# An instruction order made anew: a planner's durations and gaps as a trace shows them, and the 1e-9 of a softmax on ScalarE or VectorE

## The chip, the cores and the metric

The kernel runs on one core of a Trainium2 chip. The metric is the device time of one execution in microseconds (us). The kernel before takes 829.24 us, the median of three runs that lie between 827.79 and 829.8. The execution whose profile is read here took 828.89 us.

The engines are called as in the profile: PE is TensorE (PEld its weight loads), ACT is ScalarE, DVE is VectorE, POOL is GpSimd, and SP is SyncE, which here only starts DMAs.

## The reference

Windowed attention is followed by a gated two-layer product, all in float32:

```python
# q, k, v: (8 batches, 8 heads, 576, 64); mask: 32 keys back, for heads 4..7 every 4th key of 128
scores = where(mask, (q @ k.T) / 8, -1e9)
attn = exp(scores - scores.max(-1))
attn = attn / (attn.sum(-1) + 1e-9)
x = (attn @ v) laid out as (4608 tokens, 512)
h = x @ w_in                          # (4608, 2048)
g = h * (1 / (1 + exp(-1.702 * h)))
out = g @ w_out                       # (4608, 512)
```

## The kernel before, in words

**The products.** A float32 product is made of three products in a faster format (fp32r): each operand is split into a high part and the rest, and high x high, rest x high and high x rest are added. So a step of 128 rows on a tile of 512 tokens is three matmuls of 128x512. Over the whole kernel 3168 such matmuls carry the two layers. The weights arrive as 64-bit words, 16 tiles of w_in (`wi0` to `wi15`) and 16 of w_out, and are decoded on the chip (`decode`): seven passes over each tile by ACT, DVE and POOL, the last two of them writing `wi_kept` or `wo_kept`.

**The stages.** The tokens of a batch are one group of 512 (the last 64 of all the batches make a ninth group). Three groups, m0, m1 and m2, are done plainly: for each of 16 tiles f of the hidden layer, `up` makes `hp_m`(f) with 12 matmuls, ACT and DVE gate it, ACT and DVE or POOL split it (`gh`, `gl`), and 12 matmuls add it to four accumulators `acc_m`. The other six groups are done in three blocks p, q and r of two groups each, by a scheme with seven products of sums of halves in place of eight; its matmuls are `up_p` (or q, r) and `second_p`. In a unit of a block seven products of six matmuls take turns in two PSUM banks, and ACT or DVE empties a bank before it is begun anew. Other matmuls (`acc_m`, `second`) stand between them where there are some.

**The attention.** 32 pairs of heads (four of a batch) are done by small matmuls: `scores` writes `sp`, DVE takes the maximum and subtracts it, ACT takes the exponential (`exponentials`), DVE sums it, adds 1e-9 and takes the reciprocal (`inverse`), DVE or POOL multiplies, DVE transposes in squares of 32, and `product` (for the first batch `first_product`, which writes `first_x`) multiplies by v. `drain_x` copies the result: for the first batch ACT writes the high part into `xs` and DVE the rest. The first batch's four pairs come ahead of everything else, because m0 is made from them; while they run the weights are decoded. In those first microseconds PE also gets matmuls whose results nobody uses (`idle`).

**What sets the order.** Every piece of work is given to `Plan.add` with the engines that could do it and a duration for each, a number of urgency, and what it reads and writes. `Plan.placed` then goes through time with a model of five engines, lays each piece on one of its engines, and writes down the order; `Plan.latest` works out when a piece must start so as not to hold up PE, and the placing is done again three times with these due times. The program is written out in this order, and on the chip every engine works through its own list, in order, waiting on semaphores. So the planner's durations don't set a time on the chip. They choose which engine does a piece, and what stands ahead of what.

Its rules, as far as the change touches them: an engine is free again when its piece ends; the result can be used on another engine after `LATENCY` of that engine, and on the same one 0.13 later (0 on PE). A negative duration of DVE marks a piece that can't run at the same time as one of POOL (`port`). PE's instruction list comes in blocks, which `fetched` models. `idle` matmuls are put in wherever, in the model, PE waits for over half a microsecond in the first 60 us.

Of the kernel before, what the change touches and what calls it, by code (L numbers as in the profile page):

```python
# [10 lines left out]
AF = mybir.ActivationFunctionType  # L11
# [30 lines left out]

PE, ACT, DVE, POOL, DMA = range(5)
LATER = {PE: 0.0, ACT: 0.0, DVE: 0.51, POOL: 0.04, DMA: 0.0}
LATENCY = {PE: 0.3, ACT: 0.2, DVE: 0.2, POOL: 0.2, DMA: 0.2}


class Plan:
# [62 lines left out]
    def placed(self, warm_until, soon, late=None):  # L111
# [22 lines left out]
        def fetched(count, when, cost):  # L134

            n = issued[0]
            issued[0] += count
            for j in range(len(blocks) - 1, 1 << 30):
                edge = 193 + 256 * j
                if edge >= n + count or edge > 1500:  # L140
                    return when + cost
                part = cost * (edge - n) / count
                at = max(when + part, blocks[j])
                blocks.append(at + (6.1 if at < 18.0 else 4.2))
                when, cost, n, count = at, cost - part, edge, count - (edge - n)
# [7 lines left out]
        while any(open_):  # L153
# [41 lines left out]
            starts[i] = when  # L195
            if e == PE:
                cost = fetched(ops[i][5], when, cost) - when
            if e == POOL or (e == DVE and ops[i][0][e] < 0):
                port[0] = when + cost

            free[e] = when + (cost if e != DMA else 0.7 if cost < 100 else 0.43)
            if e == DMA:
                bus[0] = max(bus[0], when + 2.0) + cost / 360.0
                cost = bus[0] - when
            for j in users[i]:
                for to in ready[j]:
                    gap = 0.0 if to == e == PE else 0.13 if to == e else LATENCY[to]
                    ready[j][to] = max(ready[j][to], when + cost + gap + ops[j][4])
                wait[j] -= 1
                if not wait[j]:  # L210
                    for to in ops[j][0]:
                        open_[to].add(j)
# [4 lines left out]
def tile_windowed_attention_then_gated_mlp(  # L217
# [130 lines left out]
    def pair(e, dst, a, b, op):  # L348
        (V if e == DVE else G).tensor_tensor(out=dst, in0=a, in1=b, op=op)  # L349
# [5 lines left out]
    def decode(n, urgency):  # L355
# [30 lines left out]
        def take_sign(e):  # L386
# [7 lines left out]
        add({ACT: 0.66}, urgency, lambda e: A.activation(value, f32(at["top"]), AF.Copy, scale=2.0 ** -112), (R,), (E,))  # L394
        add({ACT: 0.66}, urgency, lambda e: A.activation(
            at["low"], at["low"], AF.Copy, scale=2.0 ** -29), (R,), (R + "l",))
        add({DVE: -0.75, ACT: 1.37}, urgency, take_sign, (R,), (R + "l",))
        add({DVE: -0.43}, urgency, lambda e: V.tensor_scalar(
            out=word, in0=word, scalar1=3, scalar2=None, op0=ALU.logical_shift_left), (), (E,))
        add({DVE: -0.70, POOL: 1.33}, urgency, lambda e: pair(e, word, word, at["low"], ALU.add), (R + "l",), (E,))  # L400
# [106 lines left out]

    def inverse(k, urgency):
        sm, SM = sms[turn(k)], f"sm{turn(k)}"
        add({DVE: -0.15}, urgency, lambda e: V.tensor_scalar(  # L510
            out=sm, in0=sm, scalar1=1.0e-9, scalar2=None, op0=ALU.add), (), (SM,))
        add({DVE: 0.19}, urgency, lambda e: V.reciprocal(out=sm, in_=sm), (), (SM,))  # L512

    def softmax(k, urgency):

        y = turn(k)
        pr, sm, ct = prs[y], sms[y], cts[y]
        PR, SM, CT = (f"{n}{y}" for n in ("pr", "sm", "ct"))
        exponentials(k, urgency)
        add({DVE: 0.80}, urgency, lambda e: V.tensor_reduce(out=sm, in_=pr, axis=AX.X, op=ALU.add), (PR,), (SM,))  # L520
        inverse(k, urgency)
        for a in range(2):
            add({POOL: 0.85, DVE: -0.48}, urgency, lambda e, a=a: pair(
                e, pr[:, a], pr[:, a], sm[:, a, :, None].broadcast_to([P, QT, W]), ALU.mult), (SM,), (f"{PR}.{a}",))
        if k < NC:

            for a in range(2):
                to = ct.rearrange("p h t a q -> p (h t a q)")[:, a * QT * W:a * QT * W + QT * W]
                add({DVE: 0.48}, urgency, lambda e, a=a, to=to: V.transpose(
                    out=to, in_=pr[:, a].rearrange("p t w -> p (t w)")), (PR, f"{PR}.{a}"), (f"{CT}.{a}",))  # L530
            return
        for half in (0, 1):
            add({DVE: 0.42}, urgency, lambda e, half=half: V.transpose(  # L533
                out=ct[:, half].rearrange("p t a q -> p a t q"), in_=pr[:, :, :, 32 - 32 * half:64 - 32 * half]),
                (PR, f"{PR}.0", f"{PR}.1"), (f"{CT}.{half}",))

        for m in range(8):
            j, prev = m % 4, m // 4  # L540
            odd, upper = j % 2, j // 2
            row = D * upper + 32 * (odd != prev)
            col = 32 * odd if not prev or odd else 64
            shift = prev and not odd
            tiles = slice(1 if shift and not upper else 0, QT - upper)
            to = slice(1, QT) if upper and not shift else slice(0, tiles.stop - tiles.start)
            dst = bt[row:row + 32, to, :, col:col + 32]
            src = ct[32 * j:32 * j + 32, prev, tiles]

            def work(e, dst=dst, src=src):  # L550
                if e == DMA:
                    load(dst, src)
                else:
                    copy(e, dst, src)

            costs = {DMA: 82} if k < FIRST * NC else {ACT: 0.49, DVE: -0.33}
            add(costs, urgency, work, (f"{CT}.{prev}",), (f"bt.{m}",))

    def first_product(k):
# [732 lines left out]
```

## Time and profile before

| what | us |
|---|---|
| median of three runs | 829.24 (827.79 to 829.8) |
| the profiled execution | 828.89 |
| its span, first to last instruction | 827.2 |
| PE busy | 811.2 (98%) |
| DVE busy | 669.7 (81%) |
| ACT busy | 515.0 (62%) |
| POOL busy | 327.8 (40%) |
| mean busy share of the DMA queue q1 | 69.3% |

The span is 1.7 us shorter than the execution's time. A share of busy time is a mean over stages: PE is idle for 7.9 us of the first 40 and for 4.8 us of the last 27, and hardly anywhere else. Matmuls overlap, and their ends are modelled, so a wait of PE begins earlier than the idle time that a row shows.

### The profile page before, as it was taken

To read this page: it belongs to the slowest core of one execution; us is meant where nothing else is said; L and a number is where in the kernel's file an instruction comes from. 1 tells how busy PE (TensorE), PEld (TensorE's weight loads), DVE (VectorE), ACT (ScalarE), POOL (GpSimd) and SP (SyncE) were. 2 spreads that over 40 slices of the span, in tenths; PEclk is the share of its full clock that TensorE was granted. 3 is DMA by queue.
4 is the path that set the end of the run, shared out by engine and by line. 5 is a ranking of instruction groups with operands and counts; after the bars stand their busy time and mean duration, and the time that the engine had idled before them with its cause. 6 is when DMAs were issued, how large, how long until landed. Compare 5 with 4: busy or idle time off the path is not lost.

```text
span 827.2 us, 18837 instructions
## 1 busy us (share of the span) xinstructions
PE 811.2 (98%) x7240; PEld 653.5 (79%) x7240; DVE 669.7 (81%) x1104; ACT 515.0 (62%) x992; POOL 327.8 (40%) x296
## 2 busy tenths in 40 slices
PE   7899999999999999999999999999999999999997
PEld 4678777888878888878788788888888888888886
DVE  6898989787888778898989998977679876867575
ACT  7998986676676777586776655446446544544340
POOL 3343336566655663324235357331125431112251
PEclk8799999999999999999999999999999999999999
DMA  9476658889757567868878878675665658664546
GB/s 359 152 244 193 181 192 287 295 281 314 249 189 254 183 200 257 267 190 280 279 229 261 261 233 260 219 269 168 214 193 182 211 186 273 203 222 149 189 151 181
DMA packets 109610, 188.12 MB, mean 227 GB/s; under 512 B 26448, under 2 KB 55376, under 8 KB 109520
## 3 DMA queue, kind: packets, MB, share of 16 engines
q1 hardware_dynamic: 109376, 186.78, 69.3%
q8 instruction: 57, 0.93, 0.5%
q14 instruction: 33, 0.27, 0.1%
q10 hardware_dynamic: 144, 0.13, 0.0%
HBM read 140.64 MB, written 45.09 MB: 225 GB/s over the span
## 4 chain that ended last, share of the span: by engine, by line
PE 88%; DVE 7%; ACT 1%; issue 1%; DMA 1%; SPq 0%; DVEq 0%; ACTq 0%
PE hp_m L848 15%; PE up_q L991 9%; PE up_r L991 9%; PE up_p L991 8%; PE second_q_Q L1106 5%; PE second_r_Q L1106 5%; PE second_p_Q L1106 5%; PE acc_m L785 5%; PE acc_m L789 5%; PE acc_m L786 4%; PE sp L482 3%; PE second_r_Z L1106 3%; PE second_R L1106 3%; PE second_q_Z L1106 3%; PE second_p_Z L1106 2%; PE av L607 2%
## 5 line engine op out<-in xcount | busy, mean ns | idle before, releaser
L349 POOL TENSOR_TENSOR arena<-arena 128x256 f32<-128x256 f32 (+3 forms) x109 | 118.0, 1091 | 155.7 <-DVE wi_last_units L349 34.7
L848 PE MATMUL hp_m<-xs,wi_kept 128*128 128x512 f32 x504 | 129.1, 398 | 0.7 <-DVE xs L349 0.4
L848 PEld LDWEIGHTS hp_m<-xs,wi_kept 128*128 128x128 f32 x504 | 93.3, 188 | 22.5 <-DVE arena L857 1.6
L342 ACT ACTIVATE wo_kept<-arena 128x512 fp32r<-128x512 f32 x115 | 71.9, 629 | 42.3 <-PE second_r_Q L1106 11.4
L349 POOL TENSOR_TENSOR wo_kept<-arena,wo_kept 128x512 fp32r<-128x512 f32 x34 | 45.3, 1340 | 105.5 <-ACT wo_kept L342 72.2
L991 PE MATMUL up_p<-wi_kept,xs 128*128 128x512 f32 x336 | 84.7, 394 | 2.2 <-DVE arena L349 1.3
L991 PE MATMUL up_r<-wi_kept,xs 128*128 128x512 f32 x336 | 85.3, 389 | 0.0
L991 PE MATMUL up_q<-wi_kept,xs 128*128 128x512 f32 x336 | 83.4, 389 | 0.0
L991 PEld LDWEIGHTS up_p<-wi_kept,xs 128*128 128x128 f32 x336 | 62.1, 188 | 16.8 <-DVE arena L349 2.2
L991 PEld LDWEIGHTS up_q<-wi_kept,xs 128*128 128x128 f32 x336 | 63.0, 188 | 13.4 <-DVE arena L1013 0.3
L991 PEld LDWEIGHTS up_r<-wi_kept,xs 128*128 128x128 f32 x336 | 63.1, 188 | 13.1
L349 DVE TENSOR_TENSOR wo_kept<-arena,wo_kept 128x512 fp32r<-128x512 f32 x87 | 65.3, 761 | 5.9 <-ACT wo_kept L342 5.4
L349 POOL TENSOR_TENSOR wo_kept<-wi_last_units,wo_kept 128x512 fp32r<-128x512 f32 x23 | 31.9, 1388 | 84.6 <-ACT wo_kept L342 84.6
L785 PE MATMUL acc_m<-gh,wo_kept 128*128 128x512 f32 x156 | 61.7, 395 | 0.4 <-ACT arena L342 0.3
L786 PE MATMUL acc_m<-gh,wo_kept 128*128 128x512 f32 x156 | 60.9, 390 | 0.0
L349 POOL TENSOR_TENSOR pr<-pr,sm 128x320 f32<-128x320 f32 x52 | 43.3, 850 | 43.0 <-DVE sm L512 29.3
L342 ACT ACTIVATE bt<-ct 32x256 f32<-32x256 f32 (+1 forms) x127 | 55.2, 435 | 3.2 <-DVE ct L533 0.9
L1012 ACT ACTIVATE arena<-arena 128x512 f32<-128x512 f32 x60 | 37.5, 628 | 28.9 <-DVE arena L349 25.1
L349 DVE TENSOR_TENSOR gl<-arena,gh 128x512 fp32r<-128x512 f32 x53 | 44.9, 847 | 9.1 <-PE acc_m L789 6.4
L349 DVE TENSOR_TENSOR arena<-arena 128x512 f32<-128x512 f32 (+1 forms) x68 | 50.4, 747 | 0.4
L1013 DVE SCALAR_TENSOR_TENSOR arena<-arena 128x512 f32<-128x512 f32 x60 | 48.1, 807 | 0.7 <-ACT arena L1012 0.2
L342 ACT ACTIVATE wo_kept<-wi_last_units 128x512 fp32r<-128x512 f32 x47 | 29.6, 629 | 30.0 <-PE second_r_Z L1106 8.9
(261 smaller groups left out, 1826.6 us busy)
## 6 DMA issues: line engine op xcount, KB each, us to landing
xs<-sums SPq DMA_DIRECT2D x168, 256.0 KB, 3.3
out_weights<-sums_o SPq DMA_DIRECT2D x63, 512.0 KB, 3.8
qk<-qk_dram SPq DMA_DIRECT2D x29, 576.0 KB, 5.2
xs<-sums_o SPq DMA_DIRECT2D x21, 512.0 KB, 3.6
v<-vp_dram SPq DMA_DIRECT2D x28, 320.0 KB, 4.4
sums<-arena SPq DMA_DIRECT2D x32, 256.0 KB, 3.6
sums_o<-arena SPq DMA_DIRECT2D x32, 256.0 KB, 3.4
arena<-wi_dram SPq DMA_DIRECT2D x15, 512.0 KB, 4.7
```

Source lines behind the costliest of these rows:

```text
L342: A.activation(dst, src, AF.Copy, scale=scale)
L349: (V if e == DVE else G).tensor_tensor(out=dst, in0=a, in1=b, op=op)
L482: T.matmul(dst[:, w:w + n], u["qk"][rows, at:at + 32], u["qk"][rows, S + first:S + first + n], start=not masked(k), stop=True, tile_positi ...
L607: T.matmul(u["x"][i][rows, at:at + last - first], u["v"][keys, a, m], bt[keys, m, a, first:last], start=(bank_, a) not in begun, stop=True ...
L785: T.matmul(self.acc[j], w[:, 0, cols], high, start=f == 0, stop=False)
L786: T.matmul(self.acc[j], w[:, 1, cols], high, start=False, stop=False)
L789: T.matmul(self.acc[j], w[:, 0, P * j:P * j + P], low, start=False, stop=f == NF - 1)
L848: T.matmul(hps[f], wi(f)[:, st, cols], mv[:, c], start=c == 0 and k == 0, stop=c == NC - 1 and k == 2)
L991: T.matmul(self.banks[place], xs[:, slot, at:at + P], wi_kept[:, 2 * a + c, mv], start=fresh and c == 0 and k == 0, stop=c == 1 and k == 2 ...
L1012: add({ACT: 0.60}, -10.0, lambda e: A.activation(unit(tmp), src(), AF.Tanh, scale=0.851), need, own(tmp))
L1013: add({DVE: -0.70 if need[0][0] == "A" else 0.70}, -10.0, lambda e: V.scalar_tensor_tensor(out=unit(dst), in0=unit(tmp), scalar=1.0, in1=s ...
L1106: T.matmul(self.second[key], w[:, st, cols], mv, start=fresh and y == 0 and k == 0, stop=y == 1 and k == 2, skip_group_check=True)
```

## The change

The planner's numbers are changed, and with them the order of all five engines' lists. Results are handed on sooner in the model (`LATENCY`, with exceptions in `FROM`), and ACT, DVE and POOL are free for their next piece a little before a piece ends (`LEAVES`). The durations of some pieces are set anew. And the addition of 1e-9 to the sums of a softmax, which DVE alone could do, may be done by ACT too, as a copy with a bias.

```diff
 LATER = {PE: 0.0, ACT: 0.0, DVE: 0.51, POOL: 0.04, DMA: 0.0}
-LATENCY = {PE: 0.3, ACT: 0.2, DVE: 0.2, POOL: 0.2, DMA: 0.2}
+LATENCY = {PE: 0.06, ACT: 0.04, DVE: 0.04, POOL: 0.09, DMA: 0.2}
+FROM = {PE: {ACT: 0.2, DVE: 0.2}, DMA: {PE: 0.3, ACT: 0.2, DVE: 0.2, POOL: 0.2}}
+LEAVES = {PE: 0.0, ACT: 0.10, DVE: 0.085, POOL: 0.045, DMA: 0.0}
...
+            leaves = when + cost - min(LEAVES[e], 0.6 * cost)
             if e == POOL or (e == DVE and ops[i][0][e] < 0):
-                port[0] = when + cost
-
-            free[e] = when + (cost if e != DMA else 0.7 if cost < 100 else 0.43)
+                port[0] = leaves
+
+            free[e] = leaves if e != DMA else when + (0.7 if cost < 100 else 0.43)
...
-                    gap = 0.0 if to == e == PE else 0.13 if to == e else LATENCY[to]
+                    gap = 0.0 if to == e == PE else FROM.get(e, {}).get(to, LATENCY[to])
...
-        add({DVE: -0.75, ACT: 1.37}, urgency, take_sign, (R,), (R + "l",))
+        add({DVE: -0.65, ACT: 1.22}, urgency, take_sign, (R,), (R + "l",))
...
-        add({DVE: -0.15}, urgency, lambda e: V.tensor_scalar(
-            out=sm, in0=sm, scalar1=1.0e-9, scalar2=None, op0=ALU.add), (), (SM,))
+        def shift(e):
+            if e == ACT:
+                A.activation(sm, sm, AF.Copy, bias=1.0e-9)
+            else:
+                V.tensor_scalar(out=sm, in0=sm, scalar1=1.0e-9, scalar2=None, op0=ALU.add)
+
+        add({ACT: 0.2, DVE: -0.15}, urgency, shift, (), (SM,))
...
-            add({POOL: 0.85, DVE: -0.48}, urgency, lambda e, a=a: pair(
+            add({POOL: 0.73, DVE: -0.48}, urgency, lambda e, a=a: pair(
...
-                add({DVE: 0.48}, urgency, lambda e, a=a, to=to: V.transpose(
+                add({DVE: 0.50}, urgency, lambda e, a=a, to=to: V.transpose(
...
-            add({DVE: 0.42}, urgency, lambda e, half=half: V.transpose(
+            add({DVE: 0.50}, urgency, lambda e, half=half: V.transpose(
...
-            costs = {DMA: 82} if k < FIRST * NC else {ACT: 0.49, DVE: -0.33}
+            costs = {DMA: 82} if k < FIRST * NC else {ACT: 0.45, DVE: -0.29}
```

Over the whole program the amount of work is the same but for `idle` matmuls of 128x512, of which there are 30 before and 12 now. Work moves between engines: 31 of the 32 additions of 1e-9 go from DVE to ACT; of the additions, subtractions and products of two tiles (the helper `pair`) DVE has 514 before and 554 now, and POOL 286 and 246; of the copies (`copy`) ACT has 726 and 742, and DVE 63 and 49. Three places show how the order moves; a row is a line, an operation, and what it writes and reads, and `x3` means three alike in a row.

**PE at the end of the first batch's attention**, from the first matmuls of m0 to the fourth pair's product (`hp_m_0` is tile f = 0 of m0, `first_x` the first batch's attention). Before:

```order
L848 MATMUL hp_m_0_556<-xs,wi_kept 128x512 x3
L1237 LDWEIGHTS ident
L1237 MATMUL idle<-ident 128x512
...
L575 MATMUL first_x<-ct_91,arena 64x64 x24
...
L848 MATMUL hp_m_0_556<-xs,wi_kept 128x512 x3
L848 MATMUL hp_m_1_623<-xs,wi_kept 128x512 x6
...
L575 MATMUL first_x<-ct_92,arena 64x64 x24
```

With the change:

```order
L858 MATMUL hp_m_0_559<-xs,wi_kept 128x512 x3
L858 MATMUL hp_m_1_567<-xs,wi_kept 128x512 x3
L585 MATMUL first_x<-ct_91,arena 64x64 x24
...
L858 MATMUL hp_m_0_559<-xs,wi_kept 128x512 x3
L858 MATMUL hp_m_1_567<-xs,wi_kept 128x512 x3
L858 MATMUL hp_m_2_636<-xs,wi_kept 128x512 x6
L585 MATMUL first_x<-ct_92,arena 64x64 x24
```

Matmuls of m0's second and third tile have moved ahead, to where `idle` ones stood; before the fourth quarter of x is needed, 27 matmuls of m0 are listed now, and 18 before.

**ACT in the same stretch**, from the exponential of the third pair (`pr_83`) to that of the fourth (`pr_84`). Before:

```order
L506 ACTIVATE pr_83<-pr_83 128x640
L394 ACTIVATE arena<-cell_236 128x512
L395 ACTIVATE cell_236<-cell_236 128x512
L395 ACTIVATE arena<-arena 128x512 x2
L388 ACTIVATE cell_236<-cell_236 128x512
L388 ACTIVATE arena<-arena 128x512
L506 ACTIVATE pr_84<-pr_84 128x640
```

With the change (L399, L400 and L393 are L394, L395 and L388 of before; L517 is the addition of 1e-9):

```order
L511 ACTIVATE pr_83<-pr_83 128x640
L347 ACTIVATE wi_kept<-arena 128x512
L399 ACTIVATE arena<-cell_237 128x512
L517 ACTIVATE sm_88<-sm_88 128x10
L400 ACTIVATE cell_237<-cell_237 128x512
L347 ACTIVATE wo_kept<-arena 128x512
L393 ACTIVATE cell_237<-cell_237 128x512
L399 ACTIVATE arena<-arena 128x512
L400 ACTIVATE arena<-arena 128x512 x2
L393 ACTIVATE arena<-arena 128x512 x2
L511 ACTIVATE pr_84<-pr_84 128x640
```

Six pieces stood between the two exponentials; now eleven do.

**PE at the start of block p** (`av_25` is the product of pair 25, `sp_31` the scores of pair 31, the last; `up_p_2_0` is the first bank of unit 2). Before:

```order
L991 MATMUL up_p_1_0_4688<-wi_kept_68,xs_72 128x512 x3
L789 MATMUL acc_m2_3_3488<-gl1_76,wo_last_71 128x512
L991 MATMUL up_p_2_0_4799<-wi_kept_68,xs_72 128x512 x6
L991 MATMUL up_p_2_1_4819<-wi_kept_68,xs_72 128x512 x6
L991 MATMUL up_p_2_0_4799<-wi_kept_68,xs_72 128x512 x6
L607 MATMUL av_25_4843<-bt_77,v_25_4481 64x96 x2
```

With the change, where the block begins, and at its unit 2:

```order
L487 MATMUL sp_31_4995<-qk_31_4919 32x64 x36
L1001 MATMUL up_p_0_0_5035<-wi_kept_68,xs_72 128x512 x6
...
L1001 MATMUL up_p_2_0_5299<-wi_kept_68,xs_72 128x512 x6
L1001 MATMUL up_p_2_1_5311<-wi_kept_68,xs_72 128x512 x6
L1001 MATMUL up_p_2_0_5299<-wi_kept_68,xs_72 128x512 x6
L1001 MATMUL up_p_2_1_5311<-wi_kept_68,xs_72 128x512 x6
L1001 MATMUL up_p_2_0_5299<-wi_kept_68,xs_72 128x512 x6
L1001 MATMUL up_p_2_5_5358<-wi_kept_68,xs_72 128x512 x6
L1001 MATMUL up_p_2_0_5299<-wi_kept_68,xs_72 128x512 x6
```

The attention has moved ahead: all 32 pairs' scores stand ahead of block p's first matmul, where 27 stood before, and the block's matmuls stand with less between them.

## The prediction

> **What bounds the kernel now.** I read the page's busy times and chain of waits first, then the busy time by stage, then PE's own rows where it isn't busy. The first two say that PE sets the time:
>
> ```profile
> span 827.2 us, 18837 instructions
> PE 811.2 (98%) x7240; PEld 653.5 (79%) x7240; DVE 669.7 (81%) x1104; ACT 515.0 (62%) x992; POOL 327.8 (40%) x296
> ...
> PE 88%; DVE 7%; ACT 1%; issue 1%; DMA 1%; SPq 0%; DVEq 0%; ACTq 0%
> ```
>
> PE is idle for 827.2 - 811.2 = 16.0 us, and no order makes its matmuls shorter. Where that idle time lies is shown by the busy times of stretches (PE is the second number, then PEld, DVE, ACT and POOL with their counts; then the granted clock and DMA):
>
> ```profile
> 0.00:20.00 20.00, 15.05 (x469) 8.96 (x469) 12.11 (x33) 14.66 (x21) 6.74 (x15) 0.91 0.92 358
> 20.00:40.00 20.00, 17.07 (x377) 11.73 (x376) 17.22 (x36) 18.19 (x28) 8.16 (x8) 0.75 0.44 146
> ...
> 120.00:340.00 220.00, 219.28 (x2878) 176.47 (x2877) 182.93 (x323) 153.75 (x347) 123.64 (x129) 1.00 0.76 249
> ...
> 360.00:400.00 40.00, 38.41 (x380) 30.38 (x379) 34.73 (x60) 29.20 (x64) 13.33 (x12) 1.00 0.83 270
> ...
> 440.00:480.00 40.00, 39.35 (x251) 31.90 (x250) 37.51 (x58) 27.93 (x64) 17.82 (x16) 1.00 0.77 250
> 480.00:800.00 320.00, 319.68 (x1408) 263.84 (x1407) 244.45 (x362) 156.20 (x265) 101.91 (x72) 1.00 0.65 209
> 800.00:827.20 27.20, 22.41 (x99) 18.21 (x98) 16.28 (x26) 4.10 (x7) 7.08 (x5) 0.96 0.57 174
> ```
>
> 7.9 us are lost before 40 us, 4.8 at the end (the last additions and stores, whose order is the same in both lists), 1.6 and 0.65 in block p. So what an order can win is a part of the start and some 4 us in the middle. The other 1.1 us are spread over some 680, in which there is more to lose than to win.
>
> **The change part by part. The start.** PE's rows of the first batch's attention (start, duration, what; in brackets the idle time ahead and what ended it):
>
> ```profile
> 16.02 0.40 PE L482 MATMUL sp<-arena 64*32 64x64 f32 x21 [1.76 <-issue]
> ...
> 20.27 0.44 PE L482 MATMUL sp<-arena 64*32 64x64 f32 x9
> 22.31 1.37 PE L482 MATMUL sp<-arena 64*32 64x64 f32 x75 [1.60 <-issue]
> 23.61 1.18 PE L575 MATMUL first_x<-ct,arena 32*64 32x32 f32 x53
> 25.70 0.91 PE L575 MATMUL first_x<-ct,arena 32*64 32x64 f32 x39 [0.90 <-issue]
> ```
>
> Three waits of 1.76, 1.60 and 0.90 us are put down to "issue": no engine ended them. From the first to the second of them PE ran 127 matmuls (the 21 and the 9 shown, and 97 in the rows left out), from the second to the third 75 + 53 = 128, that is, with a weight load each, 256 instructions. So PE's own instructions arrive in blocks here, 6.3 and 3.4 us apart. Taking out idle matmuls (7, 9 and 3 become 5, 6 and 1) moves these borders five to seven matmuls further down the list, still inside the same products of the third and fourth pair. I take nothing for it, within 0.3 us either way.
>
> Behind the third border the chain runs through x:
>
> ```profile
> 26.61 1.58 PE hp_m L848 x3
> 28.19 1.31 PE idle L1237 x3
> 29.49 1.17 PE first_x L575 x62
> ...
> 38.18 0.96 PE hp_m L848 x3
> ```
>
> The third pair's product waits for three idle matmuls; now three of `hp_m` stand there, at the same half speed (1.58 for three), so nothing is won in time at this place, but the work is useful. Against this ACT now has eleven pieces, not six, between the exponentials of the third and fourth pair:
>
> ```profile
> 20.08 0.79 ACT L506 ACTIVATE pr<-pr 128x640 f32<-128x640 f32 x1
> 20.77 0.65 ACT L394 ACTIVATE arena<-cell 128x512 f32<-128x512 f32 x1
> 21.32 0.65 ACT L395 ACTIVATE cell<-cell 128x512 uint32<-128x512 uint32 x1
> ...
> 22.98 1.34 ACT L388 ACTIVATE cell<-cell 128x512 f16<-128x512 f32 x1
> 24.06 1.41 ACT L388 ACTIVATE arena<-arena 128x512 f16<-128x512 f32 x1
> 25.76 0.74 ACT L506 ACTIVATE pr<-pr 128x640 f32<-128x640 f32 x1 [0.29 <-DVE pr L349]
> ```
>
> From start to start an L388 takes 1.1 us and the others 0.55. Before: 4 x 0.55 + 2 x 1.1 = 4.4, with 0.3 of waiting 4.7. Now: 7 x 0.55 + 3 x 1.1 + 0.2 for the addition = 7.3, so that the fourth exponential starts near 27.8. Behind it on ACT stands the copy of the second pair's x, which the third pair's product must wait for: its start goes from 29.5 to about 30.1. It ends ahead of two more rounds of ACT and DVE, in which DVE has one piece more ahead of the last split of x, and so the fourth quarter of x comes some 1.2 us later than 38.18. But 27 matmuls of m0 are done by then, and not 18: 9 x 0.227 (1.36 us for six) = 2.0 us. **Start: -0.8 us**, between -2 (the copy isn't late) and +1.2 (the early matmuls themselves wait for their weights).
>
> **The 1e-9.** 31 of 32 additions leave DVE:
>
> ```profile
> L510 DVE TENSOR_SCALAR sm<-sm 128x10 f32<-128x10 f32 x32 | 7.9, 247 | 0.4
> L349 DVE TENSOR_TENSOR wo_kept<-wi_last_units,wo_kept 128x512 fp32r<-128x512 f32 x25 | 17.8, 711 | 5.2 <-ACT wo_kept L342 5.0
> L349 POOL TENSOR_TENSOR wo_kept<-wi_last_units,wo_kept 128x512 fp32r<-128x512 f32 x23 | 31.9, 1388 | 84.6 <-ACT wo_kept L342 84.6
> ```
>
> DVE is freed of up to 7.9 x 31/32 = 7.7 us. No row shows ACT on 128x10. The smallest ACT form near it takes 0.23 (64 columns), and below its fixed part it can't fall, so 31 x 0.2 = 6 us on an engine at 62%. The softmax's chain goes once more to ACT and back; that lies beside PE's matmuls everywhere but in the start, where it is in the sum above. Nothing for the time.
>
> **From POOL to DVE** go 40 pieces of two tiles: 40 x 0.71 = 28 us more on DVE, 40 x 1.39 = 56 less on POOL; with the 1e-9 and the copies DVE stands near 685 of 827. Half of them are splits in blocks p to r, where DVE has 320 - 244 = 75 us to spare from 480 to 800. Where DVE is already full it costs time, and the tightest place is the middle of m0, while weights are still being decoded:
>
> ```profile
> 60.50:110.50 50.00, 49.91 (x540) 39.70 (x538) 43.87 (x76) 44.06 (x79) 18.32 (x16) 1.00 0.69 214
> ```
>
> Between `hp_m_4` and `hp_m_12` the lists hold 76 pieces for DVE before and 88 now, and 80 and 91 for ACT. 43.87 / 76 = 0.577 a piece, so 88 make 50.8 in 50.0; ACT, 3 of whose eleven are the short additions, comes to 49. **Middle of m0: +0.8 us**, between 0 (fewer collisions with POOL shorten DVE's pieces) and +3.0 (all twelve are pieces of two tiles at 0.76, the mean of the commonest such group).
>
> **Block p.** Here PE waits for DVE three times:
>
> ```profile
> 365.88 0.39 PE L789 MATMUL acc_m<-gl,wo_last 128*128 128x512 f32 x1
> 366.94 1.66 PE L991 MATMUL up_p<-wi_kept,xs 128*128 128x512 f32 x6 [0.67 <-DVE arena L349]
> 369.52 2.81 PE L991 MATMUL up_p<-wi_kept,xs 128*128 128x512 f32 x11 [0.93 <-DVE arena L1013]
> ...
> 460.79 1.43 PE L991 MATMUL up_p<-wi_kept,xs 128*128 128x512 f32 x5 [0.65 <-DVE arena L349]
> ```
>
> Start to start less 0.227 a matmul, the waits are 0.83, 1.09 and 0.81, and 0.11 more for each restart: 3.1 us. DVE is busy for 34.7 and 37.5 of 40 us there, with five pairs' attention in the block. The change moves that attention ahead into m1 and m2, where DVE is busy for 183 of 220 us, and with it a good part of what DVE was late with. But unit 2 now runs seven products with nothing between them, the pattern in which the first two waits arose. I leave one wait of 1.2 standing: **block p: -1.9 us**, between -3.1 and 0. Of the 1.1 us elsewhere I take half, since these waits have a different partner each: **-0.5**, between -1.1 and +1.
>
> **Sum:** -0.8 + 0.8 - 1.9 - 0.5 = -2.4 us on the profiled execution's 828.89, which lies 0.35 under the median: **826.5 us**.
>
> **Rivals.** *The waits only move* (33%). The order is another, but DVE is as full as before, and it is DVE that PE waits for. Without the 1.9 and the 0.5 it is 828.89 - 0.8 + 0.8 = 828.9. For it speaks that 98% leaves little; against it, that the crowding of block p is gone from the list.
>
> *No margin is left* (slower, 18%). The old numbers were longer than the trace's (the new ones take 0.085 off every piece of DVE), so results came before they were due. With true ones a piece is due when it is ready, and a collision with POOL makes PE wait. One mechanism, at DVE: in m0 the upper bound of +3.0, and in unit 2 of p two waits of 1.1 in place of one; the gain at the start is eaten by the 1.2 us that x is late. 828.89 + 3.0 + 1.2 + 0 = 833. It decides as soon as DVE's pieces between `hp_m_4` and `hp_m_12` take over 0.61 us each. Speaking for it: 88 pieces in 50 us. Against: POOL, which delays them, has less to do.
>
> *The clock stays low* (5%). Granted clock is the third number from the end:
>
> ```profile
> 26.00:28.00 2.00, 2.00 (x43) 1.34 (x30) 1.94 (x5) 1.86 (x6) 0.90 (x1) 0.50 0.81 266
> 30.00:32.00 2.00, 2.00 (x70) 1.75 (x54) 0.32 (x3) 1.31 (x2) 1.38 (x2) 1.00 0.11 39
> ```
>
> PE comes back to full clock after some 4 us of dense work. With 18 idle matmuls fewer, and a wait of 0.8 us before the third pair's product, that stretch could be broken and half speed last another 4 us: +2 us, 828.5. The Trainium skill (TensorE: Matmul & The Clock Gate, "What's actually happening") says that the clock rises after about 3.4 us of sustained work and falls after an idle window as long; by that rule, as an estimate, one missed window would cost 1.7 us. The trace's 4 us agree.
>
> *Nearly all waits go* (12%): -2.0 at the start, -3.1 in p, -1.1 elsewhere, nothing lost in m0: 822.7.
>
> **How the numbers follow.** My forecast has 32%. 0.3% is 2.5 us, about what a measurement of this kernel can tell from no change; measured from 829.24 "faster" ends at 826.8. Faster: the forecast and the rival that goes further, 44%. The same: waits that only move, and the clock's case, 38%. Slower: 18%. The range reaches from 821.5 (the lowest sum, 822.7, less the 1.1 us by which the fastest run lies under the profiled one) almost to the slower rival, 832.5; the likeliest case's own is 823 to 828.5.
>
> **What would show it.** Right: the first `acc_m` of m0 no later than 42.8 us with 42 matmuls of `hp_m` ahead of it (36 by 41.9 before); the fourth exponential near 27.8; DVE over 95% busy from 60 to 110; PE idle under 1.2 us in 340 to 480. Wrong: waits of PE between 60 and 340 that add up to over 2 us, waits for ACT anywhere, or PE's busy time outside the first 40 us changed by more than a microsecond.

## The result, and the profile after

The changed kernel takes 854.33 us, the median of five runs between 851.09 and 855.12. The kernel before, timed beside it, takes 828.93. The ratio is 1.030, with a 95% interval from 1.028 to 1.032: 25.4 us slower, where I had forecast 826.5 and had put the end of the range at 832.5. One run of the kernel u_bt below took 904.64 us, at a granted clock of 0.85 where the others had 0.99, and is left out of its numbers.

The page of the changed kernel, first the totals and then the shares of the chain of waits:

```profile
span 853.4 us, 18791 instructions
...
PE 815.8 (96%) x7222; PEld 652.9 (77%) x7222; DVE 681.3 (80%) x1097; ACT 527.1 (62%) x1039; POOL 276.1 (32%) x256
...
PE 61%; DVE 13%; ACT 8%; DMA 3%; issue 3%; SPq 1%; DVEq 0%; ACTq 0%
```

The span is 26.2 us longer. PE is idle for 853.4 - 815.8 = 37.6 us where it was 16.0, so 21.6 of them are new waits; 4.6 are longer busy time, in spite of 18 idle matmuls fewer. The shares of busy time of DVE and ACT hardly differ from before (81% and 62%). What differs is the chain: 88% of it was PE, and now DVE and ACT hold 21%.

Where the idle time lies is shown by the same stretches as before (span, PE, PEld, DVE, ACT, POOL; then the granted clock):

```profile
0.00:20.00 20.00, 11.86 (x462) 7.58 (x462) 14.38 (x34) 15.18 (x25) 7.65 (x16) 0.95 0.93 356
20.00:40.00 20.00, 16.47 (x366) 12.67 (x365) 15.10 (x29) 17.52 (x30) 10.74 (x11) 0.62 0.46 159
60.50:110.50 50.00, 47.70 (x458) 36.96 (x458) 46.87 (x84) 47.52 (x85) 15.67 (x15) 1.00 0.67 207
120.00:340.00 220.00, 208.48 (x2876) 164.37 (x2876) 178.46 (x296) 160.62 (x377) 122.97 (x128) 0.98 0.76 249
...
360.00:400.00 40.00, 38.87 (x458) 29.86 (x457) 29.73 (x57) 31.77 (x73) 9.63 (x10) 1.00 0.76 246
440.00:480.00 40.00, 40.00 (x178) 33.11 (x177) 29.91 (x47) 18.60 (x31) 6.51 (x5) 1.00 0.62 191
480.00:800.00 320.00, 316.70 (x1389) 259.53 (x1388) 256.17 (x382) 158.17 (x270) 69.02 (x48) 1.00 0.66 210
800.00:853.40 53.40, 47.86 (x210) 38.92 (x208) 34.63 (x52) 13.28 (x22) 9.87 (x7) 0.98 0.52 158
```

| stretch, us | PE idle before | PE idle after |
|---|---|---|
| 0 to 40 | 7.9 | 11.7 |
| 60.5 to 110.5 | 0.1 | 2.3 |
| 120 to 340 | 0.7 | 11.5 |
| 360 to 400 and 440 to 480 | 2.2 | 1.1 |
| 480 to 800 | 0.3 | 3.3 |
| 800 to the end | 4.8 | 5.5 |

The stretches are of time, and the program is up to 26 us later in them. By place: block p's first matmul is at 342.5 us before and at 373.0 after. From 40 us to there PE's idle time grew from 0.8 to 15.9 us; in block p itself (to 483.9, and to 504.7) it fell from 2.25 to 1.2. Half of the new idle time is between 120 and 340 us, in m1 and m2, where PE had next to no waits before. The view of waits names the partner (us in total, times, the longest):

```profile
PE hp_m L858 <- DVE arena L867: 14.4, 18, 2.3
PE sp L475 <- DVE pr L354: 4.3, 3, 2.0
PE second_p_Q L1116 <- DVE arena L1137: 2.5, 2, 2.1
...
PE up_p L1001 <- ACT arena L347: 0.7, 2, 0.4
```

The 14.4 us for `hp_m` lie between 40 us and the end of m2, and are most of what was lost there. The 4.3 for `sp` belong to the first 20 us, and the 2.5 for `second_p_Q` lie behind 480 us.

`hp_m` is the result of `up`, one PSUM bank for all but two of the 48 tiles. The matmuls of tile f + 1 may not begin until ACT's tanh (L866) and then DVE's gate (L867) have read tile f out of it. Who waits for whom in this chain is shown by the view of one tile, `hp_m`, before (each row: what came last, idle us of the waiting engine, times; the last row is PE waiting):

```profile
  PE hp_m L848: 26.9, 25
  ACT arena L856: 15.1, 21
...
  PE hp_m L848: 0.2, 1
```

and after (37.0 is PE's 14.4, the last row, and 22.6 of its weight loads):

```profile
  DVE arena L867: 37.0, 41
  ACT arena L866: 7.7, 14
...
  PE hp_m L858: 0.8, 1
...
  PE hp_m L858: 14.4, 18
```

Before, in 25 of 48 tiles ACT stood idle until PE had finished the tile: the tanh was next in its list and ready to go, 1.1 us early on the mean. With the change that is so in one tile. In the others ACT or DVE has another piece running when the tile is done, or waits for one, and PE waits behind it, 18 times. In 6 of them ACT idled, 6.3 us in all, until DVE had split `gl` off the tile before (in the kernel before 5 times, 2.4 us): that piece reads `g32`, into which the tanh writes, and there is one `g32`.

Two of these places. At 142 us it is ACT in part (start, duration, engine and line; the rows are ACT's, then DVE's, POOL's and PE's):

```profile
142.05 0.33 ACT L347 ACTIVATE arena<-sp 128x192 f32<-128x192 f32 x1 [2.46 <-DVE arena L354]
142.28 3.15 ACT L347 ACTIVATE bt<-ct 32x320 f32<-32x320 f32 x7
145.45 0.60 ACT L866 ACTIVATE arena<-hp_m 128x512 f32<-128x512 f32 x1
...
139.64 1.78 DVE L354 TENSOR_TENSOR arena<-arena 128x512 fp32r<-128x512 f32 x1
141.34 0.68 DVE L354 TENSOR_TENSOR arena<-sp,mask 128x512 f32<-128x512 f32 x1
...
146.08 0.69 DVE L867 SCALAR_TENSOR_TENSOR arena<-arena,hp_m 128x512 f32<-128x512 f32 x1 [0.27 <-ACT arena L866]
...
139.13 1.74 POOL L354 TENSOR_TENSOR arena<-arena 128x512 fp32r<-128x512 f32 x1
...
143.72 0.84 PE L799 MATMUL acc_m<-gl,wo_last 128*128 128x512 f32 x3
146.82 3.02 PE L858 MATMUL hp_m<-xs,wi_kept 128*128 128x512 f32 x8 [2.26 <-DVE arena L867]
```

Seven `bt` copies of the attention stand ahead of the tanh. They start (145.45 - 142.28) / 7 = 0.453 us apart. The planner takes 0.45 for one and then 0.10 off by `LEAVES`: 0.35. So it believed the tanh would start 0.7 us earlier than it could. That is a third of the 2.26 us that PE waits. Ahead of the copies ACT had idled 2.46 us for a piece of DVE (141.34), and that one stood behind another which took 1.78 us beside POOL, where the planner has at most 0.70.

At 246 us it is DVE (DVE's rows, POOL's, PE's):

```profile
245.92 1.22 DVE L354 TENSOR_TENSOR gl<-arena,gh 128x512 fp32r<-128x512 f32 x1
247.06 1.35 DVE L354 TENSOR_TENSOR arena<-arena,mx 128x640 f32<-128x640 f32 x1
248.34 1.22 DVE L354 TENSOR_TENSOR arena<-wo_last 128x512 f32<-128x512 f32 x1
249.47 0.68 DVE L867 SCALAR_TENSOR_TENSOR arena<-arena,hp_m 128x512 f32<-128x512 f32 x1
...
245.53 6.12 POOL L354 TENSOR_TENSOR arena<-arena 128x256 f32<-128x256 f32 x6
...
250.21 0.96 PE L858 MATMUL hp_m<-xs,wi_last 128*128 128x512 f32 x3 [1.45 <-DVE arena L867]
```

Three pieces of DVE take 249.47 - 245.92 = 3.55 us while POOL works beside them; in the planner they take 0.70 + 0.80 + 0.70 less three times 0.085, that is 1.95. The gate is 1.6 us later than the planner has it, and PE waits 1.45.

### The profile page after: what moved, and what is told of

Its sections match the earlier page's. It is cut to its first block, busy times and chain, and to the rows that moved or that the text cites. A ratio compares the mean times of both kernels' runs of the same rounds, so it can differ in the third digit from the quotient of the medians.

```text
span 853.4 us, 18791 instructions
## 1 busy us (share of the span) xinstructions
PE 815.8 (96%) x7222; PEld 652.9 (77%) x7222; DVE 681.3 (80%) x1097; ACT 527.1 (62%) x1039; POOL 276.1 (32%) x256
## 4 chain that ended last, share of the span: by engine, by line
PE 61%; DVE 13%; ACT 8%; DMA 3%; issue 3%; SPq 1%; DVEq 0%; ACTq 0%
PE up_r L1001 9%; PE up_p L1001 7%; PE up_q L1001 7%; PE hp_m L858 5%; PE second_q_Q L1116 5%; PE second_r_Q L1116 4%; PE second_p_Q L1116 4%; ACT bt L347 3%; DVE arena L354 3%; PE second_q_Z L1116 3%; PE second_R L1116 3%; PE second_r_Z L1116 2%; ACT arena L347 2%; PE second_p_Z L1116 2%; PE sp L487 2%
## 5 line engine op out<-in xcount | busy, mean ns | idle before, releaser
L354 POOL TENSOR_TENSOR arena<-arena 128x256 f32<-128x256 f32 (+3 forms) x99 | 105.9, 1079 | 150.2 <-DVE wi_last_units L354 62.6
L858 PE MATMUL hp_m<-xs,wi_kept 128*128 128x512 f32 x504 | 138.5, 413 | 13.7 <-DVE arena L867 12.9
L1001 PE MATMUL up_p<-wi_kept,xs 128*128 128x512 f32 x336 | 82.7, 392 | 0.8 <-ACT arena L347 0.7
L354 DVE TENSOR_TENSOR wo_kept<-arena,wo_kept 128x512 fp32r<-128x512 f32 x100 | 73.2, 745 | 10.4 <-ACT wo_kept L347 9.3
L1001 PEld LDWEIGHTS up_p<-wi_kept,xs 128*128 128x128 f32 x336 | 62.3, 188 | 15.8 <-ACT arena L347 2.3
L347 ACT ACTIVATE bt<-ct 32x256 f32<-32x256 f32 (+1 forms) x137 | 59.6, 435 | 9.5 <-DVE ct L543 5.5
L354 POOL TENSOR_TENSOR wo_kept<-arena,wo_kept 128x512 fp32r<-128x512 f32 x21 | 28.4, 1355 | 111.5 <-ACT wo_kept L347 83.7
L354 DVE TENSOR_TENSOR arena<-arena 128x512 f32<-128x512 f32 (+1 forms) x76 | 58.3, 771 | 4.2 <-ACT arena L347 2.9
L1023 DVE SCALAR_TENSOR_TENSOR arena<-arena 128x512 f32<-128x512 f32 x60 | 45.1, 757 | 10.3 <-ACT arena L1022 10.0
L354 DVE TENSOR_TENSOR wo_kept<-wi_last_units,wo_kept 128x512 fp32r<-128x512 f32 x44 | 31.3, 711 | 25.6 <-ACT wo_kept L347 24.3
L347 ACT ACTIVATE gh<-arena 128x512 fp32r<-128x512 f32 x58 | 36.8, 634 | 18.6 <-DVE arena L867 8.1
```

What stands on the lines that cost most here:

```text
L347: A.activation(dst, src, AF.Copy, scale=scale)
L858: T.matmul(hps[f], wi(f)[:, st, cols], mv[:, c], start=c == 0 and k == 0, stop=c == NC - 1 and k == 2)
L1001: T.matmul(self.banks[place], xs[:, slot, at:at + P], wi_kept[:, 2 * a + c, mv], start=fresh and c == 0 and k == 0, stop=c == 1 and k == 2 ...
L1023: add({DVE: -0.70 if need[0][0] == "A" else 0.70}, -10.0, lambda e: V.scalar_tensor_tensor(out=unit(dst), in0=unit(tmp), scalar=1.0, in1=s ...
```

## The experiments

The theory with which I began: **free too early**. `LEAVES` lets filler be laid closer ahead of the gate of `hp` than the chip can do it. Rivals: **handed on too soon** (`LATENCY` and `FROM`), **the `bt` copies alone**, **the durations or ScalarE's 1e-9**, and **any other order** (the order of before was a lucky draw). In the table every kernel is compared with runs of the kernel before on the same chip. "hp waits" is what PE waited for the gate, "tanh ready" what ACT idled until PE had finished the tile, both in us and times, in the profiled run.

| kernel | us | ratio to before, 95% interval | hp waits | tanh ready |
|---|---|---|---|---|
| before | 828.93 | | 0.2, 1 | 26.9, 25 |
| changed | 854.33 | 1.030 (1.028 to 1.032) | 14.4, 18 | 0.8, 1 |
| u_leaves | 837.5 | 1.010 (1.008 to 1.012) | 3.2, 6 | 10.3, 13 |
| u_latency | 845.87 | 1.021 (1.019 to 1.023) | 6.9, 10 | 9.1, 7 |
| u_bt | 846.43 | 1.022 (1.020 to 1.023) | 9.9, 13 | 3.4, 5 |
| c_after62 | 855.17 | 1.032 (1.029 to 1.035) | 13.5, 18 | 5.7, 3 |
| a_leaves | 841.86 | 1.015 (1.013 to 1.016) | 5.4, 7 | 8.6, 8 |
| u_both | 827.72 | 0.998 (0.997 to 1.000) | 0.5, 2 | 22.6, 23 |
| cut_after | 844.72 | 1.019 (1.017 to 1.021) | 10.2, 15 | 1.0, 2 |
| cut_before | 827.03 | 0.997 (0.995 to 0.998) | none | 26.6, 25 |
| u_dve | 845.73 | 1.021 (1.019 to 1.022) | 9.9, 12 | 1.8, 5 |
| u_bt_dve | 840.15 | 1.013 (1.012 to 1.015) | 7.0, 8 | 10.8, 8 |
| a_dur | 823.25 | 0.993 (0.992 to 0.994) | 0.4, 1 | 16.5, 22 |
| mix | 829.66 | 1.001 (1.000 to 1.002) | 0.6, 1 | 19.0, 19 |
| g_pe | 832.64 | 1.004 (1.003 to 1.006) | 1.1, 2 | 8.8, 14 |
| g_rest | 833.93 | 1.006 (1.004 to 1.008) | 0.8, 3 | 13.6, 15 |
| a_latency | 837.41 | 1.010 (1.008 to 1.011) | 4.5, 4 | 14.9, 15 |
| a_shift | 828.55 | 0.999 (0.998 to 1.000) | none | 19.2, 25 |
| c_before62 | 832.28 | 1.004 (1.002 to 1.006) | 1.5, 3 | 17.7, 24 |
| a_dur62 | 823.32 | 0.993 (0.991 to 0.995) | 1.0, 1 | 15.8, 21 |

**One part undone, and one draw more.** u_leaves:

```diff
-LEAVES = {PE: 0.0, ACT: 0.10, DVE: 0.085, POOL: 0.045, DMA: 0.0}
+LEAVES = {PE: 0.0, ACT: 0, DVE: 0, POOL: 0, DMA: 0.0}
```

> The changed kernel with LEAVES at zero: in the planner an engine is free again only when its piece ends; the handing-on times, the durations and ScalarE's 1e-9 stay as changed. Theory 'free too early' (the 0.10 and 0.085 us that the planner now takes off each piece of ACT and DVE are not there on the chip for short copies and for pieces that meet POOL, so that filler is laid ahead of the gate of hp and makes PE wait): 826 to 832 us. Rival 'handed on too soon' (the smaller LATENCY does it): still 842 to 854. Rival 'any other order costs as much': 842 or more. Rival 'bt copies alone': about 836 to 845, since the 0.45 then stands in full.

u_latency, the handing-on times of before:

```diff
-LATENCY = {PE: 0.06, ACT: 0.04, DVE: 0.04, POOL: 0.09, DMA: 0.2}
-FROM = {PE: {ACT: 0.2, DVE: 0.2}, DMA: {PE: 0.3, ACT: 0.2, DVE: 0.2, POOL: 0.2}}
+LATENCY = {PE: 0.3, ACT: 0.2, DVE: 0.2, POOL: 0.2, DMA: 0.2}
+FROM = {e: {e: 0.13} for e in (ACT, DVE, POOL, DMA)}
```

> The changed kernel with the handing-on times of before (LATENCY 0.3 and 0.2, and 0.13 on the same engine); LEAVES, the durations and ScalarE's 1e-9 stay. Theory 'free too early': most of the loss stays, 840 to 850 us. Rival 'handed on too soon': 826 to 832. Rival 'any other order costs as much': about 854.

u_bt:

```diff
-            costs = {DMA: 82} if k < FIRST * NC else {ACT: 0.45, DVE: -0.29}
+            costs = {DMA: 82} if k < FIRST * NC else {ACT: 0.54, DVE: -0.29}
```

> The changed kernel with one number different: ACT's duration of a bt copy is 0.54 and not 0.45, so that the planner lays these copies 0.44 apart, as the trace shows them, and not 0.35. Theory 'free too early', with DVE as the larger part: 846 to 852 us. Rival 'bt copies alone': 828 to 838. Rival 'handed on too soon' and rival 'any other order': 850 to 858.

c_after62:

```diff
-AHEAD = 0.58
+AHEAD = 0.62
```

> A control: the changed kernel with the planner's AHEAD at 0.62 and not 0.58, which draws another order and belongs to no part of the change. Theory 'free too early', and every theory that names a part of the change: 848 to 860 us. Rival 'the order is a matter of luck': over 8 us away from the changed kernel's 854.

Measured: 837.5, 845.87, 846.43 and 855.17 us. One other draw of the changed order costs the same, so the loss doesn't belong to that one order. `LEAVES` is the largest part, 854.3 - 837.5 = 16.8, but my theory had said that all of it would go: 837.5 is above its 832, and where the rival "`bt` copies alone" had put it. u_bt decides against that rival: the copies alone are worth 7.9, as theory had it. The handing-on times have 8.5 of their own. The waits for the gate shrink in step: 14.4 to 3.2, 6.9 and 9.9.

**Both undone, one alone, and the same order with a faster DVE.** u_both joins the diffs of u_leaves and u_latency:

> The changed kernel with LEAVES at zero and the handing-on times of before: what is left of the change are the durations and ScalarE's 1e-9. With LEAVES at zero alone it took 837.5. Theory 'free too early and handed on too soon' (both take margin out of the order): 827 to 832 us. Rival 'durations or the 1e-9' for the remaining 8.5 us: 835 to 840.

a_leaves is the kernel before with the changed `LEAVES` and the three lines of `placed` that use it:

> The kernel before with LEAVES alone: the planner takes 0.10 us off each piece of ACT, 0.085 off DVE's and 0.045 off POOL's before the engine is free again; the handing-on times, durations and the 1e-9 on DVE are those of before. Theory 'free too early': at least half of the changed kernel's loss, 841 to 852 us. Rival 'the parts only hurt together' (the old handing-on times still hold a margin): 828 to 836.

cut_after and cut_before keep their order and shorten pieces of DVE:

```diff
+CUT = slice(0, 384)
...
-                out=g32, in0=g32, scalar=1.0, in1=hps[f], op0=ALU.add, op1=ALU.mult), (place,), ("g32",))
+                out=g32[:, CUT], in0=g32[:, CUT], scalar=1.0, in1=hps[f][:, CUT], op0=ALU.add, op1=ALU.mult), (place,), ("g32",))
...
-            def work(e, cols=slice(0, GT)):
+            def work(e, cols=CUT):
```

(and the same in the gates of the blocks, L1023, and in one step of `decode`).

> The changed kernel, its order as it is, with some 250 pieces of DVE shortened: the gates, one step of the decode and the additions to the result work on 384 of their 512 columns, so about 0.14 us less each, 35 us or 5% of DVE's time (the output is wrong for it; PE, ACT and POOL do what they did). Theory 'no slack at DVE' (the order is right for a DVE that is a little faster than the chip's): PE's waits go, 828 to 840 us. Rival 'the order itself is bad', whatever DVE takes: 850 or more. Rival 'ACT's bt copies set it': 848 or more.

> The same pieces shortened in the kernel before, its order as it is. Theory 'no slack at DVE', which says that the order of before has slack to spare: 826 to 829 us, within 3 us of the kernel before. If DVE's work costs time everywhere: 815 to 823.

Measured: u_both 827.72, a_leaves 841.86, cut_after 844.72, cut_before 827.03. u_both settles where the loss is: with both margins back nothing of it is left, and the tanh is ready in 23 tiles. Its hp_m view (ACT idle for PE; PE waiting):

```profile
  PE hp_m L858: 22.6, 23
...
  PE hp_m L858: 0.5, 2
```

`LEAVES` put into the kernel before costs 12.5 us by itself, at the lower end of what theory gave it. The cut shows the same from the chip's side. DVE's busy time is 32 us less in cut_after:

```profile
PE 812.9 (96%) x7222; PEld 652.3 (77%) x7222; DVE 649.4 (77%) x1097; ACT 527.0 (63%) x1039; POOL 277.9 (33%) x256
```

and its hp_m view (DVE idle for ACT's tanh; PE waiting for the gate) reads:

```profile
  ACT arena L866: 8.3, 15
...
  PE hp_m L858: 10.2, 15
```

The cut wins 9.6 us in the changed order (854.33 to 844.72) and 2.3 in that of before (from 829.36 beside it to 827.03): the changed order hands a delay of DVE on to PE, and the old one swallows most of it. But 844.72 is outside the 828 to 840 of "no slack at DVE", and under what its rivals gave. PE still waits 10.2 us for a gate that is itself shorter, and DVE idles for a late tanh as long as before the cut (8.3 us, and 7.7). So this cut of DVE's work takes away somewhat over a third of the loss, not all.

**Which engine's lead, and are right means enough.** u_dve sets `LEAVES` of DVE alone to 0; u_bt_dve does that and gives ACT's `bt` copy 0.55 us, so 0.45 after the lead:

> The changed kernel with LEAVES of DVE alone at zero; ACT keeps its 0.10, POOL its 0.045, the handing-on times stay as changed. LEAVES at zero for all took 837.5, and 5% less work for DVE with the order kept 844.7. Theory 'DVE's lead is the larger part': 838 to 844 us. Rival 'ACT's lead' (bt copies and all that stands ahead of a tanh): 847 to 854.

> The changed kernel with two numbers set to what DVE and ACT take on the mean: LEAVES of DVE at zero (its pieces take longer where they meet POOL) and 0.55 for ACT's bt copy. The short handing-on times stay. Theory 'two wrong means' (with right means the order needs no margin): 827 to 832 us. Rival 'an order needs a margin whatever the means' (LEAVES at zero left 8.5 us, which only the longer handing-on times took away): 835 to 842.

a_dur is the kernel before with the new durations alone (0.65 and 1.22, 0.73, 0.50 twice, 0.45 and 0.29). mix has durations, ScalarE's 1e-9 and the handing-on times of before:

```diff
-AHEAD = 0.58
+AHEAD = 0.62
...
-LEAVES = {PE: 0.0, ACT: 0.10, DVE: 0.085, POOL: 0.045, DMA: 0.0}
+LEAVES = {PE: 0.0, ACT: 0.01, DVE: 0.01, POOL: 0.01, DMA: 0.0}
```

> The kernel before with the new durations alone (sign pass, POOL's product, transposes, bt copies); LEAVES, LATENCY and the 1e-9 as before. Theory 'the loss is in LEAVES and LATENCY' : 825 to 831 us, nothing lost by the durations. Rival 'the new bt duration (0.45 for 0.49) costs by itself': 833 or more.

> A version to beat both: the durations and ScalarE's 1e-9 of the change, the handing-on times of before, LEAVES at 0.01 for ACT, DVE and POOL, and AHEAD at 0.62. If durations and 1e-9 are harmless and margins stay, 822 to 828 us; if any other draw costs by chance, over 832.

Measured: 845.73, 840.15, 823.25 and 829.66. DVE's lead is worth 8.6 us, about as much as the cut of its work, and 845.73 lies between the two ranges that I had given; with the `bt` copies it is 14.2, most of what `LEAVES` has. So two wrong means were in the numbers, and 11 us of loss remain with both mended: "two wrong means" (827 to 832) falls, and "a margin whatever the means" (835 to 842) stands. mix, meant to beat both kernels, doesn't beat the one before: 829.66 lies between its two ranges and decides nothing.

a_dur does, by 5.6 us, and so by more than the 825 to 831 I had expected. Block p gained. The stretch from 340 to 480 us, in the kernel before and then in a_dur:

```profile
340.00:480.00 140.00, 137.75 (x1211) 110.80 (x1210) 124.63 (x207) 96.98 (x207) 51.12 (x45) 1.00 0.77 249
```

```profile
340.00:480.00 140.00, 139.94 (x1292) 113.21 (x1291) 120.72 (x200) 99.39 (x209) 61.30 (x51) 1.00 0.77 257
```

2.25 us of idle time there became 0.06. But the gain isn't to be read from that alone: over the whole span PE's idle time fell by 0.8 only (16.0 to 822.5 - 807.3 = 15.2), as the first 40 us lost 1.2. The other 3.9 us are shorter busy time of PE (811.2 to 807.3), with 26 `idle` matmuls in place of 30; what else is in it I didn't trace.

**What is left: the handing-on times, the 1e-9, and luck.** g_pe and g_rest are u_leaves with a part of the old handing-on times:

```diff
 # g_pe
+LATENCY = {PE: 0.3, ACT: 0.04, DVE: 0.04, POOL: 0.09, DMA: 0.2}
 # g_rest
+LATENCY = {PE: 0.06, ACT: 0.2, DVE: 0.2, POOL: 0.2, DMA: 0.2}
+FROM = {DMA: {PE: 0.3, DMA: 0.13}, ACT: {ACT: 0.13}, DVE: {DVE: 0.13}, POOL: {POOL: 0.13}}
```

> The changed kernel with LEAVES at zero (837.5 us) and of the handing-on times only PE's put back to 0.3; to ACT, DVE and POOL they stay short. Theory 'the hand-over to PE' (the next tile of hp is planned 0.24 us sooner behind its gate, so filler may stand closer ahead of the gate): 827 to 832 us. Rival 'the hand-overs among ACT, DVE and POOL': 835 to 840. If each has its share: 831 to 835.

> The changed kernel with LEAVES at zero and the handing-on times to ACT, DVE and POOL put back to 0.2 (0.13 on the same engine); PE's stays at 0.06. Theory 'the hand-over to PE': 835 to 840 us. Rival 'the hand-overs among ACT, DVE and POOL': 827 to 832. If each has its share: 831 to 835.

a_latency and a_shift are the kernel before with one part of the change each, the two lines of the handing-on times and the function `shift`:

> The kernel before with the short handing-on times alone; LEAVES, durations and the 1e-9 as before. If the margins add up one by one: about 836 to 840 us (829 and the 8.5 to 10 that putting them back won). If one margin is enough and only both gone hurt: 827 to 832.

> The kernel before with the 1e-9 on ACT or DVE alone. If it is harmless, as I had it: 827 to 831 us. If it costs what lies between durations alone (823.25) and durations with it (827.7): 832 to 835.

Measured: 832.64, 833.93, 837.41 and 828.55. Of the 9.8 us between u_leaves and u_both PE's 0.24 has 4.9 and the others 3.6: each has its share. Short handing-on times cost 8.4 us by themselves, and not at the gate alone (4.5 us there): the profile of a_latency has PE idle for 3.8 us between 480 and 800, where it was 0.3 before. The 1e-9 on ACT is harmless by itself.

The controls, `AHEAD` at 0.62 in the kernel before and in a_dur:

> A control: the kernel before with AHEAD at 0.62 in place of 0.58. If a redraw of the order of before costs and wins little: 827 to 831 us. If it moves the time by as much as the new durations did: under 826 or over 832.

> The kernel before with the new durations alone, and AHEAD at 0.62. If the 5.6 us belong to the durations: 821 to 825 us. If they were the luck of that order: 826 to 831.

Measured: 832.28 and 823.32. A redraw can cost 3.4 us, which is more than I had given it, so sums of single parts hold to about that much. The gain of the durations came again in the second draw, to 0.1 us. With the 1e-9 beside them it was gone in both draws: u_both took 827.72 for a_dur's 823.25, and mix 829.66 for a_dur62's 823.32 (mix has a small `LEAVES`, too). Whether the 1e-9 costs something beside the new durations is left open.

## Why the prediction was wrong, point by point

**The step that failed** is the term "elsewhere -0.5", with its bounds of -1.1 and +1. I had said of those 680 us that there was more to lose than to win, and then priced the loss at 1 us, because PE's waits there were small. The right row to look at was not PE's but ACT's: `PE hp_m L848: 26.9, 25`. It says how early the tanh was, and so how much lateness the chain through the one bank of `hp` can take. I never asked what the new rules do to that reserve. Between 40 us and block p PE's idle time grew by 15.1 us, nearly all of it waits for the gate. Of the 21.6 us of new idle time the start has 3.8, the middle of m0 2.2 and the end 0.7, and block p gave back 1.05; so some 16 lie in what I had called elsewhere and put at -0.5. The 3.0 among them from 480 to 800 are not of this ring: there PE waits for other pieces of DVE (ahead of `second_p_Q`, `second_r_Q` and `up_q`).

**The slower rival** had the right sentence, "with true ones a piece is due when it is ready, and a collision with POOL makes PE wait", and u_leaves, u_both and cut_after show it at work. Its place and size were wrong: I looked at the middle of m0 and at unit 2 of block p and came to 833. It is in all of m0 to m2, and DVE's lead is a third of it (8.6 of the 26.6 us between the changed kernel and u_both); most of the rest is ACT's copies and the shorter gaps, which I hadn't priced. Its condition didn't hold either: from 60.5 to 110.5 DVE took 46.87 / 84 = 0.558 a piece, under my 0.61, and over the same tiles (60.36 to 114.93) 51.03 / 90 = 0.567. So the mean load didn't decide this; in the two places above it was what stood just ahead of the tanh and the gate. 18% was too little for a change that takes a margin off every piece. The rivals that ended level or faster fell with the forecast.

**The start, -0.8.** The fourth exponential is at 27.52, for 27.8, with some luck: ACT's eleven pieces took 7.4 us, for 7.3, but the third exponential began at 19.51 and not at 20.08, and 20.77 + 7.3 would have been 28.1. The timeline of the changed kernel, ACT's row and some of PE's:

```profile
27.52 0.78 ACT L511 ACTIVATE pr<-pr 128x640 f32<-128x640 f32 x1
...
31.32 4.79 PE L858 MATMUL hp_m<-xs,wi_kept 128*128 128x512 f32 x12
36.03 1.08 PE L585 MATMUL first_x<-ct,arena 32*64 32x64 f32 x80
...
40.50 1.89 PE L858 MATMUL hp_m<-xs,wi_kept 128*128 128x512 f32 x7 [0.66 <-DVE xs L354]
...
44.76 0.39 PE L795 MATMUL acc_m<-gh,wo_kept 128*128 128x512 f32 x1
```

But the first `acc_m` is at 44.76, not by 42.8, with the 42 matmuls ahead of it: 2.8 later than before for 6 x 0.227 = 1.4 us more work, so 1.4 us lost and not 0.8 won. The rival that had 5%, the clock, came true here. From 30 to 34 us (before, then after) the granted clock is 1.00 and 0.50:

```profile
30.00:34.00 4.00, 4.00 (x79) 2.85 (x62) 2.32 (x6) 3.31 (x6) 1.38 (x2) 1.00 0.06 22
```

```profile
30.00:34.00 4.00, 4.00 (x86) 3.43 (x87) 2.38 (x5) 4.00 (x6) 2.17 (x3) 0.50 0.43 137
```

Twelve matmuls of `hp_m` take 4.79 us there, 0.40 each, which at 0.227 would be 2.7: my +2 us for it was the right size. The fourth pair's product stands behind them. It begins at 36.03, for 34.00 before, and the last quarter of x comes 2.3 us later (40.50 for 38.18), where I had 1.2. That the missing `idle` matmuls kept the clock low isn't shown: no run puts them back alone. Nor had I priced the waits of the first 20 us: PE waits 4.3 us for DVE ahead of `sp` there, for 0.4 before.

**The 1e-9, nothing:** right by itself. 31 on ACT take 0.212 each, where I took 0.2, and a_shift is 0.999 (0.998 to 1.000).

**POOL to DVE, the middle of m0, +0.8 with +3.0 as the bound:** 2.2 us more idle time from 60.5 to 110.5, in the bounds, towards the upper one. DVE is busy for 94% of it, not over 95%, and ACT for 95%.

**Block p, -1.9:** right in direction and within its bounds, but nearer to half of it. The three waits of `up_p` for DVE (0.67, 0.93 and 0.65 in the rows before) are gone, and 0.7 us for ACT is what the view of waits has there now; PE's idle time in the block fell by 1.05. From 340 to 480 us, where the end of m2 now lies, too, it is 1.9 and not under 1.2. The gain was lost many times over elsewhere.

**The signs against it** that I named were the right ones: waits between 60 and 340 us beyond 2 us (some 14), waits for ACT, and PE's busy time outside the first 40 us (8.4 us longer there, 4.6 in all; part of it is work that PE did earlier before, and the clock was low behind two stalls, below).

## What to carry to other kernels

In a list schedule whose engines run in order, a duration or a gap that is too long is not only an error: it is the margin that lets a late piece arrive before it is needed, and where a single buffer goes round between three engines (here one bank: matmul, tanh, gate, matmul) its lateness is paid by the engine that sets the time. Before taking margin out, look in the profile of before at how long the *hidden* engines stand idle, ready, in that ring: 26.9 us in 25 of 48 tiles was the reserve, and it fell to 0.8. It is a sign and not a price: a_dur has 16.5 and is the fastest, a_latency has 14.9 and loses 8.4 us. And set the mean of a piece, with its collisions, from start to start: 0.085 off each DVE piece doesn't hold beside POOL, where at 246 us three pieces took 3.55 us for 1.95. Right means alone weren't enough here, as u_bt_dve shows; the margin is a number of its own.

## What the runs showed of the hardware

ACT's next piece begins before the last one's end by an amount that depends on the piece. The addition of 1e-9 takes 0.21 us, and the next piece starts 0.12 after it begins (ACT's timeline in the changed kernel):

```profile
21.29 0.21 ACT L517 ACTIVATE sm<-sm 128x10 f32<-128x10 f32 x1
21.41 0.66 ACT L400 ACTIVATE cell<-cell 128x512 uint32<-128x512 uint32 x1
```

The seven 32x320 copies above start 0.453 apart, and one that stands alone (at 187.78 us) takes 0.45: for them there is no lead at all. One number for an engine is wrong for one or the other.

The clock can be low behind a wait of PE of about 2 us. After the waits of 2.26 us at 146.8 and of 1.91 at 181.2 the granted clock was 0.62 and 0.59 over the next 4 us; after one of 2.15 at 506.8 it stayed at 1.00. The 4 us behind each in the changed kernel, the clock third from the end:

```profile
146.80:150.80 4.00, 3.98 (x53) 2.78 (x58) 2.69 (x5) 2.04 (x5) 1.30 (x2) 0.62 0.49 181
181.20:185.20 4.00, 4.00 (x11) 2.97 (x11) 2.55 (x4) 2.12 (x5) 1.12 (x2) 0.59 0.76 237
...
506.80:510.80 4.00, 4.00 (x18) 3.33 (x19) 4.00 (x7) 0.63 (x1) 0.47 (x1) 1.00 0.85 250
```

The length alone doesn't decide it. The Trainium skill (TensorE: Matmul & The Clock Gate, "What's actually happening") says that the clock falls after an idle window of about 3.4 us, and that the window is free-running. Two waits shorter than that stand ahead of a low clock here, so the measurement goes beyond the page; why a third of nearly the same length doesn't, no run here tests.
